# Weight decoding on Trainium2: the low bits and the sign share one word before the join

## The chip, the core and the metric

The kernel runs on one core of a Trainium2 chip. The metric is the device time of one execution in microseconds (us). The engines are TensorE (PE, with its weight loads PEld), VectorE (DVE), ScalarE (ACT), GpSimd (POOL) and SyncE (SP); transfers are issued from SP's and ACT's queues.

## The reference, cut to what matters

```python
out_up    = repeat(softmax(mean4(q) @ mean4(k).T * scale) @ mean4(v), 4)   # 4 x 8 heads, 576 tokens, 64 wide
out_local = softmax(where(abs(i - j) < 4, q @ k.T * scale, -1e9)) @ v
x = (out_up + out_local) as (2304 tokens, 512)
x = maximum(maximum(x @ w1, x @ w2), x @ w3) @ w_out      # 512 -> 768 -> 512
h = maximum(x @ w_in, 0); y = h * h @ w_out2              # 512 -> 2048 -> 512
```

q, k and v are 32-bit floats. All weights are 64-bit floats: a scale that is a 64-bit number multiplied them when they were drawn. The kernel receives them as 64-bit words.

## The kernel before, in words

**Decoding.** A weight block of 128x512 64-bit words (512 KB) is loaded into one of three buffers of the pool `stg` (tiles `raw_g` for w1 to w3, `raw_o` for the two output weights, `raw_f` for w_in; 18, 22 and 16 blocks, 56 in all). `raw_words` returns two views of it, the low and the high 32-bit words, each 128x512 at a step of 8 bytes. Then, by block:

- `rebias` (L108, DVE, one tensor operand and two constants) corrects the exponent in the high word;
- `low_bits` (L114, ACT) scales the low word so that its top three bits remain as a small integer;
- `join` issues two DVE instructions with two tensor operands each: L117 shifts the high word left by three, which drops its sign, and ors in the low bits; L120 takes the sign from the high word and ors it in. The low word now holds a 32-bit float.
- The float is split into a rounded part `hi` (ACT) and a remainder `lo` (DVE for w1 to w3, POOL for the others); each product on PE is three matmuls (`mm3`, L141 to L143: hi·hi, hi·lo, lo·hi).

**Stages.** Attention of batch 0 runs first, beside the decoding of w1 to w3; then, batch by batch, the gate units (`gate_unit`, PE into PSUM, DVE maximum `c` at L399), their output units, and the attention of the next batch. In the attention of batch b, `x32` (L352, DVE) takes the attention output of a pair of heads out of PSUM; `x3210F` is the one of batch 1, pair 0, front part. The last feed-forward block is cut into 24 units that the code calls quads: 3 token groups by 8 weight quads. In a quad PE computes seven products `P` (L141 to L143), from which DVE forms the sums `u` and `c` (L729, L737, L740, L744, L748), squares them (L714, L733) and subtracts (`gl`, L671); PE then multiplies these into `po`. `decode_quad` decodes four blocks (two `raw_f`, two `raw_o`) for one weight quad, forms four sums of them (L532 to L535) and stores the results for the later token groups; this is spread over the last batch and over the first token group, so that the quads from 465 to 568 us run beside it, and the later ones not.

**Order.** On PE the order is written by hand. On the other engines a scheduler orders the instructions at build time by a simulated timeline; at run time each engine takes its queue strictly in order, so an instruction that waits holds all behind it.

Of the kernel before, what the change touches and what calls it, by code (L numbers as in the profile page):

```python
# [7 lines left out]

F32 = mybir.dt.float32
F32R = mybir.dt.float32r  # L10
U32 = mybir.dt.uint32
U64 = mybir.dt.uint64
AF = mybir.ActivationFunctionType
ALU = mybir.AluOpType
# [7 lines left out]
LOW_BITS = 0.9375 * 2.0**-29  # L22
# [36 lines left out]
def local_global_attention__then__moe_kernel(  # L59
    ctx: ExitStack, tc: tile.TileContext, qT, kT, vP, cst, wg, wo1, wi2, wo2, out  # L60
):
    nc = tc.nc
# [38 lines left out]
    def raw_words(src, name):  # L101
        raw = stg.tile([P, 512], U64, tag="raw", name=f"raw_{name}")
        nc.sync.dma_start(out=raw, in_=src)
        words = raw.bitcast(U32).rearrange("p (n two) -> p n two", two=2)
        return words[:, :, 0], words[:, :, 1]

    def rebias(high):
        nc.vector.tensor_scalar(  # L108
            out=high.bitcast(F32), in0=high.bitcast(F32), scalar1=REBIAS, scalar2=F32_TOP,
            op0=ALU.mult, op1=ALU.min,  # L110
        )

    def low_bits(out, low):
        nc.scalar.activation(out=out, in_=low, func=AF.Copy, scale=LOW_BITS)  # L114

    def join(out, high, bits):
        nc.vector.scalar_tensor_tensor(  # L117
            out=out, in0=high, scalar=3, in1=bits, op0=ALU.logical_shift_left, op1=ALU.bitwise_or
        )
        nc.vector.scalar_tensor_tensor(  # L120
            out=out, in0=high, scalar=0x80000000, in1=out, op0=ALU.bitwise_and, op1=ALU.bitwise_or
        )

    def split_mid(items):
        parts = []
        work = [raw_words(src, name) for src, name, *_ in items]
        for (src, name, pool, tag, bufs), (low, high) in zip(items, work):
            rebias(high)
            low_bits(low, low)
            join(low, high, low)  # L130
            hi = pool.tile([P, 512], F32R, tag=tag, name=f"hi_{name}", bufs=bufs)
            lo = pool.tile([P, 512], F32R, tag=tag, name=f"lo_{name}", bufs=bufs)
            w = low.bitcast(F32)
            nc.scalar.activation(out=hi, in_=w, func=AF.Copy)
            eng = nc.gpsimd if wo_pool else nc.vector
            eng.tensor_tensor(out=lo, in0=w, in1=hi.bitcast(F32), op=ALU.subtract)
            parts.append((hi, lo))
        return parts
# [171 lines left out]
    def att_pv(b, p, part):  # L310
# [32 lines left out]
        if (b, h) not in x_t:  # L343
            assert not h or not b or all((b - 1, 1, f) in h_t for f in range(NF1))
            x_t[b, h] = (
                xp.tile([P, NP, N], F32R, tag=f"xhi{h}", name=f"xhi{b}{h}", bufs=2 - h),
                xp.tile([P, NP, N], F32R, tag=f"xlo{h}", name=f"xlo{b}{h}", bufs=2 - h),
            )
# [19 lines left out]
    def load_w1(n=2):  # L368
        keys = w1_todo[:n]
        del w1_todo[:n]  # L370
        items = [
            (wg[f, g], f"g{f}{g}", wpool, "w", 36) if kind == "g" else (wo1[f], f"o1{f}", wo_pool[0], "wo", 12)
            for kind, f, g in keys
        ]
        if items:
            w1_t.update(zip(keys, split_mid(items)))
# [16 lines left out]
    def gate_max(b, h, f, g, ps, c):  # L393
# [6 lines left out]
        if g == NG - 1:  # L400
            hhi = hp.tile([P, N], F32R, tag=f"hh{h}{f}", name=f"hh{b}{h}{f}")
            hlo = hp.tile([P, N], F32R, tag=f"hl{h}{f}", name=f"hl{b}{h}{f}")
            nc.scalar.activation(out=hhi, in_=c, func=AF.Copy)  # L403
# [76 lines left out]
    def quad_tiles(q):  # L480
        n = loads[0]
        loads[0] += 1
        t = w2_t[q] = {}
        for c in CUT:
            for e in "hl":
                if n % 4 == 3:
                    t[c + e] = gp.tile([P, 512], F32R, tag="w", name=f"w{n}{c}{e}", bufs=12)
                else:
                    t[c + e] = wpool.tile([P, 512], F32R, tag="w", name=f"w{n}{c}{e}", bufs=36)
        return t  # L490

    def split_cut(q, c, w, c0=0):
        n = w.shape[-1]
        hi, lo = w2_t[q][c + "h"][:, c0 : c0 + n], w2_t[q][c + "l"][:, c0 : c0 + n]
        nc.scalar.activation(out=hi, in_=w, func=AF.Copy)
        nc.gpsimd.tensor_tensor(out=lo, in0=w, in1=hi.bitcast(F32), op=ALU.subtract)

    def store_cut(q, c):
        n = 256 if c == "i3" else 512
        for e in "hl":  # L500
            nc.sync.dma_start(out=wscr[q][c + e], in_=w2_t[q][c + e][:, 0:n].bitcast(F32))

    def decode_quad(q):

        raw, tb = {}, {}

        def begin(key, src):
            low, high = raw[key] = raw_words(src, f"{key}_{q}")
            rebias(high)
            low_bits(low, low)  # L510

        def end(key):
            low, high = raw[key]
            join(low, high, low)
            raw[key], tb[key] = low.bitcast(F32), high.bitcast(F32)

        def both():
            quad_tiles(q)
            end("f0")
            split_cut(q, "i0", raw["f0"])  # L520

        def other():
            end("f1")
            split_cut(q, "i3", raw["f1"][:, 256:512])

        def sums():

            t1, t2 = tb["f0"][:, 0:256], tb["f0"][:, 256:512]
            t3, t4 = tb["f1"][:, 0:256], tb["f1"][:, 256:512]
            b11, b21 = raw["f0"][:, 0:256], raw["f0"][:, 256:512]  # L530
            b12, b22 = raw["f1"][:, 0:256], raw["f1"][:, 256:512]
            nc.vector.tensor_tensor(out=t1, in0=b12, in1=b11, op=ALU.subtract)  # L532
            nc.vector.tensor_tensor(out=t3, in0=b22, in1=b12, op=ALU.subtract)
            nc.vector.tensor_tensor(out=t2, in0=b22, in1=t1, op=ALU.subtract)
            nc.vector.tensor_tensor(out=t4, in0=t2, in1=b21, op=ALU.subtract)  # L535

        def last(c, key):
            end(key)
            split_cut(q, c, raw[key])

        def stores(*cuts):
            for c in cuts:
                store_cut(q, c)

        f = 2 * q
        return [
            lambda: begin("f0", wi2[f]),
            lambda: begin("f1", wi2[f + 1]),
            both,
            other,  # L550
            sums,
            lambda: (split_cut(q, "i1", tb["f0"]), begin("o0", wo2[f]), stores("i0", "i3")),
            lambda: (split_cut(q, "i2", tb["f1"]), begin("o1", wo2[f + 1]), stores("i1", "i2")),
            lambda: last("o0", "o0"),
            lambda: (last("o1", "o1"), stores("o0", "o1")),
        ]
# [275 lines left out]
```

## Time and profile before

| | |
|---|---|
| Median of 3 runs | 865.99 us (865.09 to 867.10) |
| The profiled execution | 864.85 us |
| Its span, first to last instruction | 863.1 us |
| PE busy | 809.9 us (94%) |
| DVE busy | 561.0 us (65%) |
| ACT, POOL busy | 298.5 us, 220.7 us |
| Mean granted TensorE clock | 0.972 |

The profile is read by stretches: the shares of the whole span average over a start in which PE has gaps, a long middle in which it has none, and the quads. A busy time is that of the instruction on its engine, with what it waits for a memory port included. Idle time is put down to the instruction that ended it. The granted clock is a share of full speed, where 1.0 is 2.4 GHz and 0.5 is 1.2 GHz.

### The profile page before, as it was taken

What the parts mean: (1) busy time and instruction counts of PE and PEld (TensorE: products, weight loads), DVE (VectorE), ACT (ScalarE), POOL (GpSimd) and SP (SyncE); (2) the same over time, 40 slices, a digit from 0 to 9 for tenths busy, and PEclk for the clock granted to TensorE, in tenths of its full rate; (3) what the DMA queues carried; (4) which work ended last, traced back from release to release, by engine and by line L of the source; (5) the groups of instructions that cost most, each with busy time, mean ns of one, the idle gap of its engine ahead of it and who ended that gap; (6) DMA issues with size and microseconds to landing.
All of it is one profiled execution on the core that took longest, in us unless ns stands there. A gap on an engine that the chain in (4) does not pass through costs nothing. (4 is left out here: it accounts for less than half of the span.)

```text
span 863.1 us, 15554 instructions
## 1 busy us (share of the span) xinstructions
PE 809.9 (94%) x6016; PEld 741.7 (86%) x6016; DVE 561.0 (65%) x1072; ACT 298.5 (35%) x679; POOL 220.7 (26%) x258
## 2 busy tenths in 40 slices
PE   5578997999999999999998988899999999999998
PEld 4367996999999999999998877788888898888886
DVE  7998998623764256638776998975654546544533
ACT  3455543422343123334445434424221123211211
POOL 4735383510433104103333344412000002000000
PEclk9578999999999999999999999999999999999999
DMA  8635542320223102135765766722564100654101
GB/s 246 209 105 171 162 144 73 120 66 2 73 84 94 35 27 82 32 106 195 232 231 167 281 219 244 249 92 77 194 209 155 50 1 24 207 196 134 49 1 73
DMA packets 66232, 110.30 MB, mean 128 GB/s; under 512 B 6800, under 2 KB 29680, under 8 KB 66160
## 3 DMA queue, kind: packets, MB, share of 16 engines
q1 hardware_dynamic: 61552, 104.60, 37.1%
q10 hardware_dynamic: 4608, 4.72, 1.6%
q8 instruction: 47, 0.77, 0.4%
q14 instruction: 25, 0.20, 0.1%
HBM read 76.79 MB, written 32.51 MB: 127 GB/s over the span
## 5 line engine op out<-in xcount | busy, mean ns | idle before, releaser
L141 PE MATMUL g<-xhi,hi_g 128*128 128x256 f32 (+1 forms) x576 | 175.6, 305 | 3.3 <-DVE c L399 3.2
L142 PE MATMUL g<-xlo,hi_g 128*128 128x256 f32 (+1 forms) x576 | 172.6, 300 | 1.5 <-DVE xlo L360 1.5
L143 PE MATMUL g<-xhi,lo_g 128*128 128x256 f32 (+1 forms) x576 | 172.5, 300 | 0.0
L141 PEld LDWEIGHTS g<-xhi,hi_g 128*128 128x128 f32 x576 | 111.1, 193 | 6.3 <-DVE c L399 4.9
L142 PEld LDWEIGHTS g<-xlo,hi_g 128*128 128x128 f32 x576 | 111.7, 194 | 1.7 <-DVE xlo L360 1.7
L143 PEld LDWEIGHTS g<-xhi,lo_g 128*128 128x128 f32 x576 | 110.9, 192 | 0.0
L670 ACT ACTIVATE gh<-c 128x384 fp32r<-128x384 f32 x96 | 50.3, 524 | 149.6 <-DVE c L714 133.0
L671 DVE TENSOR_TENSOR gl<-c,gh 128x384 fp32r<-128x384 f32 x96 | 62.2, 649 | 39.7 <-ACT gh L670 39.4
L399 DVE TENSOR_TENSOR c<-g,c 128x256 f32<-128x256 f32 (+1 forms) x96 | 43.5, 453 | 65.0 <-PE g L143 64.6
L141 PE MATMUL yp<-hh,hi_o 128*128 128x256 f32 (+1 forms) x192 | 58.8, 306 | 0.0
L143 PE MATMUL yp<-hh,lo_o 128*128 128x256 f32 (+1 forms) x192 | 57.5, 299 | 0.0
L142 PE MATMUL yp<-hl,hi_o 128*128 128x256 f32 (+1 forms) x192 | 57.5, 299 | 0.0
L403 ACT ACTIVATE hh<-c 128x256 fp32r<-128x256 f32 (+1 forms) x48 | 21.2, 442 | 95.0 <-DVE c L399 95.0
L714 DVE SCALAR_TENSOR_TENSOR c<-c 128x384 f32<-128x384 f32 x72 | 43.4, 604 | 1.9
L733 DVE TENSOR_TENSOR c<-c 128x384 f32<-128x384 f32 x24 | 15.7, 654 | 39.4 <-ACT c L732 39.4
L141 PEld LDWEIGHTS yp<-hh,hi_o 128*128 128x128 f32 x192 | 37.0, 193 | 0.8 <-issue 0.6
L610 POOL TENSOR_TENSOR lS<-s,hS 128x768 fp32r<-128x768 f32 x2 | 3.7, 1840 | 131.2 <-DVE u L729 115.8
L143 PEld LDWEIGHTS yp<-hh,lo_o 128*128 128x128 f32 x192 | 37.1, 193 | 0.0
L142 PEld LDWEIGHTS yp<-hl,hi_o 128*128 128x128 f32 x192 | 37.1, 193 | 0.0
L217 POOL TENSOR_TENSOR v<-v 72x256 f32<-72x256 f32 x32 | 26.0, 829 | 38.8 <-DMA v<-in_vP 38.8
L732 ACT ACTIVATE c<-P 128x384 f32<-128x384 f32 x24 | 11.8, 490 | 59.4 <-PE P L143 58.1
L405 DVE TENSOR_TENSOR hl<-c,hh 128x320 fp32r<-128x320 f32 (+1 forms) x36 | 19.9, 554 | 12.6 <-ACT hh L403 12.6
(1829 smaller groups left out, 2121.3 us busy)
## 6 DMA issues: line engine op xcount, KB each, us to landing
raw_o<-in_wo SPq DMA_DIRECT2D x22, 512.0 KB
raw_g<-in_wg SPq DMA_DIRECT2D x18, 512.0 KB
raw_f<-in_wi SPq DMA_DIRECT2D x16, 512.0 KB
k<-in_kT SPq DMA_DIRECT2D x16, 291.0 KB
q<-in_qT SPq DMA_DIRECT2D x16, 288.0 KB
v<-in_vP SPq DMA_DIRECT2D x32, 144.0 KB
out_y<-ob SPq DMA_DIRECT2D x18, 256.0 KB
vw<-in_vP SPq DMA_DIRECT2D x16, 175.0 KB
```

What stands on the lines that cost most here:

```text
L141: nc.tensor.matmul(ps, whi, xhi, start=first, stop=False, skip_group_check=more)
L142: nc.tensor.matmul(ps, whi, xlo, start=False, stop=False, skip_group_check=more)
L143: nc.tensor.matmul(ps, wlo, xhi, start=False, stop=last, skip_group_check=more)
L217: nc.gpsimd.tensor_tensor(out=v4[:, 0:2], in0=v4[:, 0:2], in1=v4[:, 2:4], op=ALU.add)
L399: nc.vector.tensor_tensor(out=c, in0=ps[:, 0:N], in1=c, op=ALU.max)
L403: nc.scalar.activation(out=hhi, in_=c, func=AF.Copy)
L405: eng.tensor_tensor(out=hlo, in0=c, in1=hhi.bitcast(F32), op=ALU.subtract)
L670: nc.scalar.activation(out=ghi, in_=c, func=AF.Copy)
L671: nc.vector.tensor_tensor(out=glo, in0=c, in1=ghi.bitcast(F32), op=ALU.subtract)
L714: V.scalar_tensor_tensor(out=c, in0=c, scalar=0.0, in1=c, op0=ALU.max, op1=ALU.mult)
L732: A.activation(out=e, in_=d, func=AF.Relu)
L733: V.tensor_tensor(out=e, in0=e, in1=e, op=ALU.mult)
```

## The change

`low_bits` now writes its three bits as a 16-bit number into the lower halfword of the low word, and a new DVE instruction with one tensor operand takes the sign bit from the upper halfword of the high word and writes it into the upper halfword of the low word. `join` is then one instruction: shift the high word left by three and or in the low word, which holds sign and low bits. The number of DVE instructions is the same: by block, one with two tensor operands (L120) is replaced with one with one tensor operand.

```diff
-    def low_bits(out, low):
-        nc.scalar.activation(out=out, in_=low, func=AF.Copy, scale=LOW_BITS)
-
-    def join(out, high, bits):
+    def low_bits(low, high):
+
+        half = lambda words, i: words.bitcast(U16)[:, :, i]
+        nc.scalar.activation(out=half(low, 0), in_=low, func=AF.Copy, scale=LOW_BITS)
+        nc.vector.tensor_scalar(
+            out=half(low, 1), in0=half(high, 1), scalar1=0x8000, scalar2=None, op0=ALU.bitwise_and
+        )
+
+    def join(low, high):
         nc.vector.scalar_tensor_tensor(
-            out=out, in0=high, scalar=3, in1=bits, op0=ALU.logical_shift_left, op1=ALU.bitwise_or
-        )
-        nc.vector.scalar_tensor_tensor(
-            out=out, in0=high, scalar=0x80000000, in1=out, op0=ALU.bitwise_and, op1=ALU.bitwise_or
+            out=low, in0=high, scalar=3, in1=low, op0=ALU.logical_shift_left, op1=ALU.bitwise_or
         )
...
-            low_bits(low, low)
-            join(low, high, low)
+            low_bits(low, high)
+            join(low, high)
...
-            low_bits(low, low)
+            low_bits(low, high)
...
-            join(low, high, low)
+            join(low, high)
```

Since the scheduler reckons with other durations, it also puts DVE's, ACT's, POOL's and SP's instructions into another order; PE's order is the same. In the changed file the lines behind the new code have numbers that are higher by three: L109 is `rebias`, L118 the new sign step, L123 the join, L355 `x32`, L402 the maximum.

DVE's queue just ahead of `x3210F`, before. `c013` and `c014` are maxima of gate units, `raw_f0_0`, `raw_f1_0` and `raw_o0_0` are blocks of weight quad 0:

```order
L534 TENSOR_TENSOR raw_f0_0_5421<-raw_f1_0_5425,raw_f0_0_5421 128x256
L108 TENSOR_SCALAR raw_o0_0_5549<-raw_o0_0_5549 128x512
L399 TENSOR_TENSOR c014_1706<-g0141_1708,c014_1706 128x320
L535 TENSOR_TENSOR raw_f1_0_5425<-raw_f0_0_5421 128x256
L117 SCALAR_TENSOR_TENSOR raw_o0_0_5549<-raw_o0_0_5549 128x512
L399 TENSOR_TENSOR c014_1706<-g0142_1722,c014_1706 128x320
L120 SCALAR_TENSOR_TENSOR raw_o0_0_5549<-raw_o0_0_5549 128x512
L352 TENSOR_TENSOR x3210F_1767<-o10F_1750,up10_1763 128x256
```

The same place now:

```order
L538 TENSOR_TENSOR raw_f1_0_5426<-raw_f0_0_5421 128x256
L277 TENSOR_TENSOR sm11B_1511<-sm11B_1511,sms11B_1528 128x350
L402 TENSOR_TENSOR c013_1649<-g0131_1651,c013_1649 128x320
L402 TENSOR_TENSOR c013_1649<-g0132_1665,c013_1649 128x320
L402 TENSOR_TENSOR c014_1706<-g0141_1708,c014_1706 128x320
L402 TENSOR_TENSOR c014_1706<-g0142_1722,c014_1706 128x320
L355 TENSOR_TENSOR x3210F_1767<-o10F_1750,up10_1763 128x256
```

The blocks of weight quad 0 have moved ahead, so that only maxima stand just before `x3210F`; in both orders 27 blocks are decoded ahead of it.

DVE's queue around the sum `u302` of the third quad (products of PE wait for it), before; `raw_o0_4` and `raw_o1_4` are blocks of weight quad 4:

```order
L733 TENSOR_TENSOR c1102_6451<-c1102_6451 128x384
L108 TENSOR_SCALAR raw_o1_4_6437<-raw_o1_4_6437 128x512
L120 SCALAR_TENSOR_TENSOR raw_o0_4_6412<-raw_o0_4_6412 128x512
L737 TENSOR_TENSOR u302_6479<-P7_02_6472,u202_6427 128x384
L117 SCALAR_TENSOR_TENSOR raw_o1_4_6437<-raw_o1_4_6437 128x512
```

The same place now:

```order
L109 TENSOR_SCALAR raw_o1_4_6438<-raw_o1_4_6438 128x512
L123 SCALAR_TENSOR_TENSOR raw_o0_4_6412<-raw_o0_4_6412 128x512
L736 TENSOR_TENSOR c1102_6453<-c1102_6453 128x384
L118 TENSOR_SCALAR raw_o1_4_6438<-raw_o1_4_6438 128x512
L740 TENSOR_TENSOR u302_6481<-P7_02_6474,u202_6428 128x384
L123 SCALAR_TENSOR_TENSOR raw_o1_4_6438<-raw_o1_4_6438 128x512
```

The rebias of `raw_o1_4` has moved ahead of `c1102`, and its sign step stands ahead of `u302`.

## Rows read from the trace of the kernel before

**Rows 1.** The page: busy time, granted clock, and the chain that ended last.

```profile
PE 809.9 (94%) x6016; PEld 741.7 (86%) x6016; DVE 561.0 (65%) x1072; ACT 298.5 (35%) x679; POOL 220.7 (26%) x258
...
PEclk9578999999999999999999999999999999999999
...
PE 31%; DVE 7%; DMA 4%; issue 2%; POOL 1%; ACT 1%; SPq 0%; DVEq 0%; POOLq 0%; ACTq 0%
```

**Rows 2.** Busy time by stretch (start:end length, each engine, PEclk, DMA share, GB/s).

```profile
20.00:40.00 20.00, 13.43 (x138) 9.99 (x136) 20.00 (x36) 10.51 (x25) 15.30 (x20) 0.50 0.64 190
...
120.00:140.00 20.00, 13.81 (x122) 12.06 (x120) 19.72 (x36) 8.06 (x19) 13.13 (x13) 1.00 0.30 105
...
480.00:520.00 40.00, 36.43 (x176) 31.15 (x175) 38.23 (x62) 17.18 (x32) 18.76 (x11) 1.00 0.68 234
520.00:560.00 40.00, 35.50 (x170) 30.00 (x169) 35.89 (x58) 17.76 (x32) 16.29 (x13) 1.00 0.71 249
...
640.00:680.00 40.00, 40.00 (x200) 35.96 (x199) 19.03 (x35) 8.24 (x16) 0.00 (x0) 1.00 0.49 158
```

**Rows 3.** The same view, two short stretches behind those.

```profile
140.00:145.00 5.00, 4.99 (x45) 4.57 (x45) 3.42 (x10) 2.19 (x9) 0.84 (x1) 0.66 0.01 2
560.00:570.00 10.00, 7.78 (x37) 6.31 (x36) 8.61 (x14) 3.75 (x7) 3.14 (x3) 1.00 0.56 174
```

**Rows 4.** PE in order of time, waits alone: start, length, instruction, [idle before <-releaser].

```profile
79.16 1.21 PE L298 MATMUL t03B<-const,sm03B 128*70 128x128 f32 x5 [3.53 <-ACT pt02B L282]
...
123.53 0.41 PE L141 MATMUL g<-xhi,hi_g 128*128 128x320 f32 x1 [0.49 <-DVE c L399]
126.19 0.41 PE L141 MATMUL g<-xhi,hi_g 128*128 128x320 f32 x1 [0.64 <-DVE c L399]
131.18 0.41 PE L141 MATMUL g<-xhi,hi_g 128*128 128x320 f32 x1 [1.20 <-DVE c L399]
139.66 0.30 PE L298 MATMUL t10B<-const,sm10B 128*70 128x128 f32 x1 [3.81 <-DVE x3210F L352]
...
502.85 0.45 PE L141 MATMUL P<-hA,w2i2h 128*128 128x384 f32 x1 [1.34 <-DVE u L737]
```

**Rows 5.** Durations by line, ns: shortest/median/longest, first and last start.

```profile
L117 DVE SCALAR_TENSOR_TENSOR raw_o<-raw_o x22: 643/694/1807, 102.3 to 565.8; 128x512 uint32<-128x512 uint32 x22
L120 DVE SCALAR_TENSOR_TENSOR raw_o<-raw_o x22: 678/688/1840, 106.1 to 567.3; 128x512 uint32<-128x512 uint32 x22
L108 DVE TENSOR_SCALAR raw_o<-raw_o x22: 416/423/1373, 99.7 to 565.2; 128x512 f32<-128x512 f32 x22
```

**Rows 6.** Busy time of line L120 alone, by stretch.

```profile
0.00:140.00 140.00, 23.05 (x27) 0.84 0.53 166
480.00:600.00 120.00, 12.62 (x16) 1.00 0.53 182
sum 600.00, DVE 47.86; mean DVE 11.97
```

**Rows 7.** Busy time of line L108 alone, in the same stretches.

```profile
0.00:140.00 140.00, 15.03 (x27) 0.84 0.53 166
480.00:600.00 120.00, 7.52 (x16) 1.00 0.53 182
sum 600.00, DVE 28.73; mean DVE 7.18
```

**Rows 8.** DVE in order of time, at a few places.

```profile
138.42 0.68 DVE L120 SCALAR_TENSOR_TENSOR raw_o<-raw_o 128x512 uint32<-128x512 uint32 x1
139.18 0.42 DVE L352 TENSOR_TENSOR x3210F<-o10F,up 128x256 f32<-128x256 f32 x1
...
501.30 0.43 DVE L108 TENSOR_SCALAR raw_o<-raw_o 128x512 f32<-128x512 f32 x1 [1.26 <-DMA raw_o<-in_wo]
```

**Rows 9.** SP's issue of a block, and ACT's first step on it.

```profile
90.25 0.33 SPq L103 DMA_DIRECT2D raw_g<-in_wg  x1
...
94.82 0.70 ACT L114 ACTIVATE raw_g<-raw_g 128x512 uint32<-128x512 uint32 x1 [2.34 <-DMA raw_g<-in_wg]
```

More of the change, by code (lines that the diff above doesn't have):

```diff
@@ L10 @@
 F32R = mybir.dt.float32r
+U16 = mybir.dt.uint16
 U32 = mybir.dt.uint32
```

## The prediction

> **What bounds the kernel now.** I read the page first, then busy time by stretch, then PE's waits in order of time, and last the durations of the lines that the change touches. PE is busy for 94% of the span [rows 1], so a step that DVE saves is worth something only where PE waits for DVE. The table by stretch shows where that is. From 20 to 40 us DVE is busy for all 20.00 us while PE has gaps, at a clock of 0.50 [rows 2]; from 120 to 140 us DVE is busy for 19.72 of 20 us and PE for only 13.81; from 480 to 560 us DVE is busy for 38.23 and 35.89 of 40 us and PE loses 3.57 and 4.50 us. In the later quads, without decoding, PE has no gap at all (40.00 of 40) and DVE is half idle [rows 2]. So three places can give time back: the start, the end of the first decoding around 120 to 140 us, and the quads beside which weight quads are decoded. The chain that ended last names DVE for 7% and DMA for 4% of the span [rows 1], more than any engine but PE.
>
> PE's waits in the second place are four: 0.49, 0.64 and 1.20 us for a maximum `c` and 3.81 us for `x3210F` [rows 4], **6.14 us** in sum. In the third, from 480 to 570 us, PE's gaps are 3.57 + 4.50 + (10 - 7.78) = **10.3 us** [rows 2, 3].
>
> **The change part by part.** *The removed step.* L120 takes 47.86 us for 56 blocks, 0.855 us each [rows 6]; its median is 0.69 us where no one disturbs it [rows 5], the rest is time in which POOL's work holds it up. 27 blocks are decoded by 140 us (23.05 us) and 16 from 480 to 600 us (12.62 us) [rows 6].
>
> *The new step.* No row shows a DVE step on 16-bit halves, or a bitwise step with one tensor operand. The nearest row is L108: one tensor operand and constants, 128x512 elements at the same step of 8 bytes, median 0.42 us and 28.73 us in all, 0.513 each [rows 5, 7]. The farthest is L117, bitwise on the same words with two tensor operands, 0.69 us by median [rows 5], 0.855 if it is held up as L120 is. I take L108, since the number of tensor operands is what parts these two rows, and keep 0.42 to 0.855 for the range. The saving on DVE is then 23.05 - 15.03 = **8.0 us** by 140 us and 12.62 - 7.52 = **5.1 us** in the quads [rows 6, 7].
>
> The excess over the median is 0.17 us for L120 (0.855 - 0.69) and 0.09 us for L108 (0.513 - 0.42), and which of the two the new step has is open [rows 5 to 7]. The Trainium skill ("SBUF — State Buffer", SBUF: two separate sides) says that DVE and GpSimd share a port pair as an exclusive lock, held for a whole instruction, both by DVE steps with two SBUF operands and by one-operand steps in the fast mode; what a blocked step waits would then depend on POOL's instruction and not on its own length. By that rule the new step costs 0.42 + 0.17 = 0.59 us as an estimate, saves 0.265 us instead of 0.34, and the sum below falls from 8.8 to about 8.2 us.
>
> *Waits.* The new step overwrites half of the word that ACT's low_bits reads, so it waits for ACT, as L117 did before it; behind it in the queue stands what stood behind L117. In the order the rebias is followed directly by the next decoding step of its block 11 times before and 14 times now. Such a place can make DVE wait for the rest of ACT's step; three more of them, some 0.3 us each (ACT's step and the sign step start with the same landing), stay below 1 us and are in the bounds. ACT's step is the same but for 16-bit output; no row shows that, and ACT, at 35% [rows 1], has room: bounds 0 and a loss of some tenths per block that lies beside DVE's queue.
>
> *Order, start to 100 us.* The scheduler fills the time it saves with the next block: up to `x3203F` 9 sign steps and 10 rebiases stand ahead where 8 second joins and 9 rebiases did, and summing medians over the queue, `x3203F` and the last `xlo` of that part stand within 0.8 us of where they stood. What PE waits for there does not come sooner. I charge **0**, with +3.5 us if the wait of 3.53 us at 79 us [rows 4] goes, and -2.5 us if blocks land too late (below).
>
> *Order, 120 to 140 us.* In both orders 27 blocks stand ahead of `x3210F`, now with nothing but maxima just before it. DVE had no idle time there to speak of, so `x3210F` can come 8.0 us sooner, more than the 6.14 us that PE waits. Then PE's own work is next. I take **5.5 us** of the 6.14, as one maximum in the row will still be waited for. Bounds: 4, and 7.8 if the stretch behind it, at a clock of 0.66 for 5 us [rows 3], runs at full clock too (5 x 0.34 = 1.7 us).
>
> *160 to 460 us.* PE has no gaps to speak of; 13 blocks get cheaper beside it: 0.
>
> *The quads.* DVE saves 5.1 / 16 = 0.32 us per block [rows 6, 7]. But at four places DVE stands idle until a block lands, as at 501.30 us, 1.26 us, right ahead of the `u` for which PE then waits 1.34 us [rows 4, 8]; what is saved ahead of such a place goes into that wait. So 12 of 16 blocks: 3.8 us. At this very place the order is worse now: behind the landing stand a join's 0.69, a `c`'s 0.55 and the sign step's 0.42 ahead of `u302`, where the join alone stood; about 1 us, which I charge by half, since the load may be issued sooner: **3.3 us** of the 10.3. Bounds: 0 and 8.
>
> The sum is 0 + 5.5 + 3.3 = 8.8 us. Against the profiled execution (864.85 us, span 863.1) that is 856.05; the median of the runs is 1.14 us above that execution, so **857.2 us** for the median, 1.0% less.
>
> **The rivals.** *Only one term comes.* The start's gain can be lost to a late attention step, or the quads' to the loads. 865.99 - 5.5 = 860.5 or - 3.3 = 862.7; say 861.5.
>
> *Both stretches cease to wait.* If DVE falls behind PE's need in both, all of 6.14 + 1.7 and most of 10.3, and some of the start, come back: some 18 us, 848. For it: without decoding, quads show no gap. Against: DVE is busy for 74.1 of the 80 us from 480; 5.1 less is 69, against PE's 71.9 [rows 2, 6, 7], so the two stay neck and neck and waits remain.
>
> *The new step is no faster.* If a bitwise step on halves runs like L117, DVE saves nothing and only the order changes: 866, plus or minus 2. The Trainium skill ("Vector Engine (DVE) Microarchitecture Reference", 5.1) lists streams with steps above 2 as not measured, which is this step's case.
>
> *Slower: blocks land too late.* Three buffers; a block's load is issued when the remainder `lo` of the third block ahead is done, and lands some 4.6 us later: issued at 90.25, first used at 94.82 after a wait [rows 9]. By medians, DVE's work between that `lo` and the rebias was 5.0 us on average and is now 4.5, at the least 3.0. DVE then waits at the head of its queue, and softmax and `xlo` steps wait behind it while PE waits for them. It decides from 0.5 us per block on (18 blocks, 9 us, eat the sum); at 0.8 us it is a loss of 5 to 6 us: 871.
>
> **How the numbers follow.** Forecast 0.50 (853 to 860 by itself), one term only 0.16, both stretches 0.10, no faster step 0.13, slower 0.11. A measurement of this kernel tells about 0.2% (1.7 us) from no change: below 864.3 is faster, above 867.7 slower. Faster: 0.50 + 0.16 + 0.10 + 0.03 of the step that is no faster = 0.79; same 0.10, the rest of it; slower 0.11. The range from 849.5 to 866.0 leaves out the slower case and most of the greatest gain.
>
> **What would show it.** The new line at 0.42 to 0.6 us by its median (right), at 0.69 or more (wrong); DVE's busy time lower by about 19 us (47.86 - 28.73). PE's wait for `x3210F` gone, and the busy time of PE in the 20 us around it near 19. The gaps of PE in the decoding quads near 7 us instead of 10.3. DVE idle for `raw_g` before 100 us, which is none now, would show the slower case at work. The prediction falls if POOL's hold on DVE grows as DVE's steps crowd, or if PE's clock in the start is granted differently.

## The result and the profile after

The changed kernel is slower: 876.66 us median of 4 runs (876.18 to 878.89), where the kernel before took 866.22 us (865.09 to 867.10, 4 runs). The ratio is 1.0142, with an interval of 1.0126 to 1.0158; the quotient of the two medians is 1.0121, a little below it. The highest run of the kernel before is 9 us under the lowest of the changed one, so the loss is clear of the noise. The forecast was 857.2 us in a range of 849.5 to 866.0, so it had the sign wrong and missed by 19.5 us. The profiled execution took 876.61 us with a span of 874.8 us, 11.7 us more than before.

The page shows where the two new steps stand. First busy time, answering [rows 1]:

```profile
PE 813.7 (93%) x6016; PEld 743.1 (85%) x6016; DVE 559.2 (64%) x1072; ACT 330.4 (38%) x679; POOL 223.4 (26%) x258
```

DVE's busy time fell by 1.8 us where 19 were expected, and ACT's rose by 31.9 us where next to nothing was. The new lines by duration (ns: shortest/median/longest, first and last start), answering [rows 5]; L117 is now ACT's `low_bits` and L118 the sign step:

```profile
L117 ACT ACTIVATE raw_o<-raw_o x22: 1346/1382/1409, 94.1 to 572.6; 128x512 uint16<-128x512 uint32 x22
...
L118 DVE TENSOR_SCALAR raw_o<-raw_o x22: 732/752/1278, 96.5 to 574.0; 128x512 uint16<-128x512 uint16 x22
L118 DVE TENSOR_SCALAR raw_g<-raw_g x18: 723/822/1682, 17.0 to 91.6; 128x512 uint16<-128x512 uint16 x18
L118 DVE TENSOR_SCALAR raw_f<-raw_f x16: 719/750/772, 124.1 to 560.4; 128x512 uint16<-128x512 uint16 x16
```

The sign step, at 0.75 us, is no cheaper than the step it replaces (0.69) [rows 5], and ACT's step has doubled, from 0.70 us [rows 9] to 1.38.

Busy time in the stretches of [rows 2, 3] (start:end length, each engine, PEclk, DMA share, GB/s):

```profile
20.00:40.00 20.00, 13.41 (x140) 10.20 (x142) 19.71 (x38) 13.20 (x27) 15.01 (x18) 0.50 0.62 184
120.00:140.00 20.00, 16.56 (x110) 15.90 (x110) 15.33 (x33) 7.98 (x14) 13.08 (x12) 0.91 0.25 89
480.00:520.00 40.00, 35.94 (x175) 30.96 (x174) 39.27 (x61) 21.47 (x30) 13.81 (x11) 1.00 0.76 265
520.00:560.00 40.00, 35.05 (x160) 27.61 (x158) 33.25 (x57) 20.90 (x32) 13.79 (x11) 1.00 0.68 236
...
560.00:570.00 10.00, 9.27 (x45) 7.84 (x45) 9.66 (x16) 5.39 (x10) 5.93 (x4) 1.00 0.44 140
```

From 120 to 140 us PE has fewer gaps than before (16.56 us busy for 13.81), but its work there comes some 2 us later (`x3210F` starts at 141.2 us, where it started at 139.18 [rows 8]). From 480 to 570 us PE's gaps are 4.06 + 4.95 + 0.73 = 9.7 us, where 10.3 stood and near 7 was forecast, but the quads start later too. A stretch of fixed times therefore says little across kernels, and three marks in PE's own work say more: the last output of attention (`o33B`), the first matmul of the quads (`P<-hA,w0i0h`) and the first that reads weight quad 4 (`P<-hA,w4i0h`). PE in order of time, start and length, at these marks, before and then after:

```profile
381.14 0.39 PE L334 MATMUL o33B<-ptd33B,vd 72*64 72x48 f32 x8
462.52 0.34 PE L141 MATMUL P<-hA,w0i0h 128*128 128x384 f32 x1
597.37 0.33 PE L141 MATMUL P<-hA,w4i0h 128*128 128x384 f32 x1
```

```profile
381.57 0.39 PE L337 MATMUL o33B<-ptd33B,vd 72*64 72x48 f32 x8
468.88 0.34 PE L144 MATMUL P<-hA,w0i0h 128*128 128x384 f32 x1
608.31 0.33 PE L144 MATMUL P<-hA,w4i0h 128*128 128x384 f32 x1
```

So of the 11.7 us, 0.4 were lost by the first mark, 87.31 - 81.38 = 5.9 between the first and the second, 139.43 - 134.85 = 4.6 between the second and the third, and 0.8 behind it. Half of the loss lies where the forecast charged 0 ("160 to 460 us ... 0"): PE had gaps of 0.4 us in the 60 us from 400 before, and has 6.1 us of them now. Busy time in that stretch, before and then after:

```profile
400.00:460.00 60.00, 59.62 (x442) 58.95 (x441) 44.47 (x77) 26.12 (x52) 19.36 (x15) 1.00 0.69 228
```

```profile
400.00:460.00 60.00, 53.91 (x396) 52.41 (x396) 39.26 (x66) 29.40 (x46) 19.83 (x15) 1.00 0.62 213
```

What happens there is seen on DVE in order of time (start, length, instruction, [idle before <-releaser]); `c` (L402) is the maximum of the gate units, for which PE waits five times in these 60 us, 5.9 us in sum:

```profile
410.11 0.43 DVE L109 TENSOR_SCALAR raw_f<-raw_f 128x512 f32<-128x512 f32 x1 [1.93 <-DMA raw_f<-in_wi]
411.52 0.76 DVE L118 TENSOR_SCALAR raw_f<-raw_f 128x512 uint16<-128x512 uint16 x1 [0.98 <-ACT raw_f L117]
412.07 0.45 DVE L402 TENSOR_TENSOR c<-g,c 128x256 f32<-128x256 f32 x1
...
418.26 1.28 DVE L118 TENSOR_SCALAR raw_o<-raw_o 128x512 uint16<-128x512 uint16 x1
419.34 0.51 DVE L402 TENSOR_TENSOR c<-g,c 128x320 f32<-128x320 f32 x1
```

The first three rows are one block: it lands, its rebias takes 0.43 us, ACT's step takes 1.39 us from the same landing, and DVE stands idle for 0.98 us at the sign step, with the maximum behind it. PE did not yet wait for this maximum; it waited 0.81 us for the next one, at 416.22 us. The other two rows show a later maximum behind a sign step of 1.28 us, and PE's wait for it is 1.41 us:

```profile
419.90 0.42 PE L144 MATMUL g<-xhi,hi_g 128*128 128x320 f32 x1 [1.41 <-DVE c L402]
```

Over the whole run, DVE's idle time ahead of L118 (the last column; busy us and mean ns stand in front of it) is 7.0 + 4.6 + 0.6 = 12.2 us for ACT alone:

```profile
L118 DVE TENSOR_SCALAR raw_o<-raw_o 128x512 uint16<-128x512 uint16 x22 | 18.2, 828 | 4.8 <-ACT raw_o L117 4.6
L118 DVE TENSOR_SCALAR raw_g<-raw_g 128x512 uint16<-128x512 uint16 x18 | 16.7, 926 | 0.7 <-ACT raw_g L117 0.6
L118 DVE TENSOR_SCALAR raw_f<-raw_f 128x512 uint16<-128x512 uint16 x16 | 12.0, 749 | 7.7 <-ACT raw_f L117 7.0 <-DVE raw_f L109 0.5
```

Before, the step that waited for ACT was the first join (L117), and it stood idle for 1.5 + 0.2 us:

```profile
L117 DVE SCALAR_TENSOR_TENSOR raw_o<-raw_o 128x512 uint32<-128x512 uint32 x22 | 20.2, 919 | 0.4 <-ACT raw_o L114 0.2
L117 DVE SCALAR_TENSOR_TENSOR raw_f<-raw_f 128x512 uint32<-128x512 uint32 x16 | 12.9, 806 | 2.0 <-ACT raw_f L114 1.5
```

Among PE's longest waits by 140 us, answering [rows 4], these are new:

```profile
28.04 1.04 PE L309 MATMUL td01F<-const,pd01F 128*72 128x128 f32 x4 [3.50 <-DVE x3200F L355]
...
46.26 0.58 PE L145 MATMUL g<-xlo,hi_g 128*128 128x256 f32 x1 [2.81 <-DVE xlo L363]
55.27 0.58 PE L145 MATMUL g<-xlo,hi_g 128*128 128x256 f32 x1 [2.29 <-DVE xlo L363]
...
129.26 0.52 PE L144 MATMUL g<-xhi,hi_g 128*128 128x320 f32 x1 [3.34 <-ACT c L400]
```

The wait for `x3210F` (3.81 us) is gone, as forecast. In its place stand waits for `x3200F` and the remainders `xlo` in the start, and one of 3.34 us for a `c` that ACT writes. They are not what the dearer steps cost. The kernel with both steps on whole words (below), which has the same order of instructions, has them too (us in total, times, longest):

```profile
PE g L145 <- DVE xlo L363: 8.3, 3, 3.2
PE td01F L309 <- DVE x3200F L355: 4.0, 1, 4.0
PE g L144 <- ACT c L400: 2.8, 1, 2.8
```

So up to 140 us the new order mostly trades one set of waits for another, whatever the steps cost.

### The profile page after: what moved, and what is told of

Its sections match the earlier page's. It is cut to its first block, busy times and chain, and to the rows that moved or that the text cites. A ratio compares the mean times of both kernels' runs of the same rounds, so it can differ in the third digit from the quotient of the medians.

```text
span 874.8 us, 15590 instructions
## 1 busy us (share of the span) xinstructions
PE 813.7 (93%) x6016; PEld 743.1 (85%) x6016; DVE 559.2 (64%) x1072; ACT 330.4 (38%) x679; POOL 223.4 (26%) x258
## 5 line engine op out<-in xcount | busy, mean ns | idle before, releaser
L402 DVE TENSOR_TENSOR c<-g,c 128x256 f32<-128x256 f32 (+1 forms) x96 | 43.6, 454 | 65.6 <-PE g L146 65.2
L674 DVE TENSOR_TENSOR gl<-c,gh 128x384 fp32r<-128x384 f32 x96 | 59.4, 619 | 39.8 <-ACT gh L673 39.7
L717 DVE SCALAR_TENSOR_TENSOR c<-c 128x384 f32<-128x384 f32 x72 | 46.2, 642 | 2.0
L117 ACT ACTIVATE raw_o<-raw_o 128x512 uint16<-128x512 uint32 x22 | 30.4, 1381 | 25.2 <-DMA raw_o<-in_wo 23.3
```

Source lines behind the costliest of these rows:

```text
L117: nc.scalar.activation(out=half(low, 0), in_=low, func=AF.Copy, scale=LOW_BITS)
L402: nc.vector.tensor_tensor(out=c, in0=ps[:, 0:N], in1=c, op=ALU.max)
L674: nc.vector.tensor_tensor(out=glo, in0=c, in1=ghi.bitcast(F32), op=ALU.subtract)
L717: V.scalar_tensor_tensor(out=c, in0=c, scalar=0.0, in1=c, op0=ALU.max, op1=ALU.mult)
```

## The experiments

Theory 1 says that the prices of the two steps are the cause: ACT's half words hold up the head of DVE's queue, and the sign step is as dear as what it replaced. Theory 2 says that the scheduler's new order is the cause, whatever the steps cost. Theory 3 blames the sign step on halves alone.

**A table of single steps.** Six of each, 128x512 elements:

> A table of single steps, six of each, without any of the layer's computation (it leaves all of it out; its time says nothing). In the changed kernel the sign step takes 0.72 to 0.75 us where 0.42 was charged, and ACT's low bits 1.35 us where 0.69 stood before. If writing half a word beside its other half is what costs, then the same step with a contiguous output of half words is near 0.42 (VectorE) and near 0.69 (ACT), and with a contiguous input but the halves as output stays at 0.72 and 1.35. If reading half words costs on VectorE, it is the other way round: contiguous output 0.72, contiguous input 0.42. If only the spacing of 8 bytes counts, the halves at a spacing of 4 bytes are near 0.42 and 0.69. The whole-word form of the sign step (the words at a spacing of 8 bytes on both sides) gives 0.42 if halves are dearer than words, and 0.7 if they are not.

Groups by line (busy us, mean ns, idle before). In the first fence, the first four are ACT's halves or bytes, by the spacing of the output: 8 bytes (L61, and L65 for single bytes), 4 bytes (L72), contiguous (L75); then ACT's whole words at 8 bytes (L59) and contiguous (L70).

```profile
L65 ACT ACTIVATE vb<-vb 128x512 uint8<-128x512 uint32 x6 | 8.0, 1333 | 0.2
...
L61 ACT ACTIVATE vb<-vb 128x512 uint16<-128x512 uint32 x6 | 7.9, 1320 | 0.0
L72 ACT ACTIVATE g<-vb 128x512 uint16<-128x512 uint32 x6 | 5.0, 828 | 0.0
...
L75 ACT ACTIVATE g<-vb 128x512 uint16<-128x512 uint32 x6 | 4.2, 692 | 0.0
L59 ACT ACTIVATE vb<-vb 128x512 uint32<-128x512 uint32 x6 | 4.1, 679 | 16.4 <-DMA vb<-in_w 16.4
...
L70 ACT ACTIVATE g<-vb 128x512 uint32<-128x512 uint32 x6 | 4.0, 660 | 0.0
```

For DVE: halves at 8 bytes on both sides (L43), contiguous input to halves at 8 bytes (L49), halves at 8 bytes to a contiguous output (L47), halves at 4 bytes on both sides (L55), contiguous words (L53), words at 8 bytes (L45), contiguous halves (L51).

```profile
L43 DVE TENSOR_SCALAR va<-va 128x512 uint16<-128x512 uint16 x6 | 4.4, 728 | 1.5 <-DMA va<-in_w 1.5
L49 DVE TENSOR_SCALAR va<-d 128x512 uint16<-128x512 uint16 x6 | 4.3, 711 | 0.0
...
L47 DVE TENSOR_SCALAR d<-va 128x512 uint16<-128x512 uint16 x6 | 2.7, 458 | 0.0
L55 DVE TENSOR_SCALAR d<-e 128x512 uint16<-128x512 uint16 x6 | 2.7, 448 | 0.0
L53 DVE TENSOR_SCALAR e<-d 128x512 uint32<-128x512 uint32 x6 | 2.6, 433 | 0.0
L45 DVE TENSOR_SCALAR va<-va 128x512 uint32<-128x512 uint32 x6 | 2.5, 412 | 0.0
L51 DVE TENSOR_SCALAR e<-d 128x512 uint16<-128x512 uint16 x6 | 1.7, 278 | 0.0
```

It is the writing of halves at a spacing of 8 bytes that costs, on both engines: on DVE 0.71 us even from a contiguous input, and 0.46 when only the input is spaced; on ACT 1.32 for 0.69. Whole words at the same spacing cost nothing extra (0.41 and 0.68), and at 4 bytes most of the price is gone (0.45 and 0.83, for 0.28 and 0.69 contiguous).

**Two by two: halves or words on each engine.** All three kernels keep the changed kernel's order of instructions. The first one undoes ACT's part:

```diff
-        nc.scalar.activation(out=half(low, 0), in_=low, func=AF.Copy, scale=LOW_BITS)
+        nc.scalar.activation(out=low, in_=low, func=AF.Copy, scale=LOW_BITS)
```

> The changed kernel with one thing undone: ACT writes the three low bits as a whole word, as in the kernel before; the sign step then overwrites the upper half. Same order of instructions on every engine as the changed kernel. Theory 1 (ACT's output of halves, 0.69 us longer a block, holds up the head of VectorE's queue): ACT's busy time falls by 32 us, and the time to 864 to 868, within 0.3% of the kernel before, as the sign step of 0.75 us is as dear as the step that the change took out. Theory 2 (the new order of instructions loses the time, whatever the steps cost): about 875, no change. Theory 3 (VectorE's sign step on halves loses it): 873 or more, as that step is left as it is.

The second one puts the sign step on whole words as well, and the third only that:

```diff
         nc.vector.tensor_scalar(
-            out=half(low, 1), in0=half(high, 1), scalar1=0x8000, scalar2=None, op0=ALU.bitwise_and
+            out=low, in0=high, scalar1=0x80000000, scalar2=None, op0=ALU.bitwise_and
         )
```

> The changed kernel with both new steps on whole words: ACT writes the three low bits as a whole word, and VectorE then writes the sign over the whole word instead of its upper half. This leaves the three low bits out of every weight. Same order of instructions as the changed kernel. It gives the price at which the prediction's sum was made, if a whole-word step costs 0.42 us: theory 1 expects the sum to hold then, 857 us (853 to 860); theory 2 (the new order) expects 872 or more; if the whole-word step also takes 0.7 us or more, theory 1 expects the time of the kernel before, 864 to 868.

> The changed kernel with VectorE's sign step on the whole word, and ACT's output of half words as changed. This leaves the three low bits out of every weight. Same order of instructions as the changed kernel. Theory 1 (ACT's 1.38 us holds up the head of VectorE's queue; the sign step's price is some 8 us of the sum): 870 (867 to 873), still slower than the kernel before. Theory 3 (the sign step on halves is what loses the time): 859 or less. Theory 2 (the order): 875. With the first two kernels it makes a table of two by two: if the parts add, the time here is that of the changed kernel plus that of whole words on both, less that of ACT on whole words alone.

The last two of these leave the three low bits out of every weight. The first row of the table was measured beside runs of the kernel before with a median of 866.22 us, the other three beside runs with 865.26 us:

| ACT writes | sign step on | us | against before, with interval |
|---|---|---|---|
| halves | halves (the change) | 876.66 | 1.0142 (1.0126 to 1.0158) |
| words | halves | 869.62 | 1.0045 (1.0029 to 1.0060) |
| halves | words | 868.97 | 1.0035 (1.0015 to 1.0054) |
| words | words | 859.60 | 0.9936 (0.9918 to 0.9954) |

Theory 1 holds in its parts. By the medians ACT's halves cost 7.0 us with the sign step on halves and 9.4 us with it on words; the sign step's halves cost 7.7 and 10.0 us. By the ratios it is 0.97% and 0.99%, and 1.07% and 1.09%, some 8 to 9 us each, with intervals of some 0.2% on each ratio: as far as these runs tell, the two parts add. Both together make 17.1 us of the 19.5 by which the forecast was off. By the traces ACT's part goes through the head of DVE's queue, as theory 1 has it: with ACT on words and all else as changed, DVE's idle time for ACT ahead of the sign step falls from 12.2 to 2.1 us, while its other waits for ACT sum to 139.4 us with halves and 141.2 with words, and PE's own waits for ACT to 11.7 and 10.7. Theory 2 as the main cause falls, since the same order gives a gain of 0.64% at the price that the sum was made with. Theory 3 falls as well: with the sign step on words and ACT on halves the kernel is still slower than before. The first kernel was expected within 0.3% of before and came out at 0.45%; some 4 us were not in theory 1. The second (expected at 853 to 860 us) and the third (867 to 873) came out within what theory 1 said.

**The same edits in the order of before.** If the sign step is written with two inputs, the scheduler keeps the order of before:

```diff
-        nc.vector.tensor_scalar(
-            out=half(low, 1), in0=half(high, 1), scalar1=0x8000, scalar2=None, op0=ALU.bitwise_and
+        nc.vector.scalar_tensor_tensor(
+            out=half(low, 1), in0=half(high, 1), scalar=0x8000, in1=half(high, 1), op0=ALU.bitwise_and, op1=ALU.bitwise_and
         )
```

> The arithmetic of the changed kernel with ACT writing whole words, and the sign step written as an instruction with two inputs (the upper half of the high word and itself): the scheduler then puts every instruction where it stands in the kernel before. So it is the kernel with ACT on whole words and the sign step on halves, in the order of before. That kernel in the changed order took 1.0045 of before. If the new order is what cost those 0.45%, this one is at 1.000 (0.998 to 1.002), provided that the step takes about the 0.7 us of the step that it replaces; if the order costs nothing and the halves do, it is at 1.004 to 1.006.

> As the run with ACT on whole words in the order of before, with ACT's output in half words as in the changed kernel, still in the order of before. In the changed order ACT's halves cost 7.0 us (876.66 against 869.62) with the sign step on halves and 9.4 us (868.97 against 859.60) with it on whole words. If that is a matter of ACT's price alone, it is 7 to 10 us here too, 1.008 to 1.012 of before. If the new order is what exposes ACT's step (the sign step right behind the rebias at the head of VectorE's queue, waiting for ACT), it is 0 to 4 us here, 1.000 to 1.005.

Measured: 887.00 us with ACT on words, 1.0227 (1.0200 to 1.0254), and 892.89 us with ACT on halves, 1.0309 (1.0285 to 1.0334). The proviso of the first expectation did not hold: with two inputs the step on halves takes about twice the 0.7 us (1.32 to 1.33 us by its medians, more on average, as the groups of the run with ACT on words show), so neither of its branches was tested.

```profile
L118 DVE SCALAR_TENSOR_TENSOR raw_o<-raw_o 128x512 uint16<-128x512 uint16 x22 | 34.3, 1558 | 0.5 <-ACT raw_o L117 0.3
L118 DVE SCALAR_TENSOR_TENSOR raw_g<-raw_g 128x512 uint16<-128x512 uint16 x18 | 27.5, 1529 | 0.0
```

The pair still says what ACT's halves cost in the order of before: 5.9 us by the medians, which lies between the two branches of the second expectation (0 to 4 and 7 to 10 us), and 0.82%, some 7 us, by the ratios. The next run asks the same with the steps of before. Besides ACT's output it edits the shift, which is the first of the two join instructions and not the second:

```diff
-        nc.scalar.activation(out=out, in_=low, func=AF.Copy, scale=LOW_BITS)
+        nc.scalar.activation(out=out.bitcast(U16)[:, :, 0], in_=low, func=AF.Copy, scale=LOW_BITS)
...
-            out=out, in0=high, scalar=3, in1=bits, op0=ALU.logical_shift_left, op1=ALU.bitwise_or
+            out=out, in0=high, scalar=3, in1=bits, op0=ALU.logical_shift_left, op1=ALU.bitwise_and
```

> The kernel before with one thing changed: ACT writes the three low bits as a half word (into the lower half of the low word). Its second join masks with the low word where it was joined with it, to keep the values finite: the weights it decodes are wrong, the steps and their order are those of before. It gives ACT's price alone. 1.008 to 1.012 of before if 0.69 us more for a block on ACT hold up what waits for ACT wherever it stands; 1.000 to 1.005 if the new order is needed to expose it. ACT's busy time should rise by 56 x 0.65 to 0.69 = 36 to 39 us, or 32 as in the changed kernel.

Measured: 871.63 us, 1.0048 (1.0026 to 1.0071), so ACT's halves alone cost 0.48%, some 4.2 us, in the order of before, and ACT's busy time rose from 298.5 to 331.7 us. That lies at the edge of the lower branch. DVE's idle time for ACT ahead of the first join grew from 1.7 to 5.9 + 2.7 + 0.7 = 9.3 us. ACT's price is thus paid in either order, 4 to 7 us in the old and 7 to 9 us in the new one. The new order is not needed for it; whether it adds to it is not shown, since the steps differ too and the intervals nearly meet.

**Where the parts fall.** The three marks of PE's work in the profiled executions (start of `o33B`, then the time to the first matmul of the quads, to the first on weight quad 4, and to the end of the span), as differences from before in us:

| kernel | to `o33B` | to the quads | to weight quad 4 | to the end | span |
|---|---|---|---|---|---|
| halves, halves (the change) | +0.4 | +5.9 | +4.6 | +0.8 | +11.7 |
| words, halves | -2.6 | +2.4 | +1.4 | +1.4 | +2.5 |
| halves, words | -1.9 | +5.6 | -0.4 | +1.2 | +4.4 |
| words, words | -3.6 | +1.6 | -2.9 | +0.8 | -4.1 |
| before, ACT on halves | +1.8 | +1.8 | +2.4 | +1.0 | +7.0 |

Each row is one execution, and the executions of one kernel spread by up to 7 us (865.29 to 872.27 for words and halves, of which the profiled one took 867.44), so a difference of 1 to 2 us in one row is not shown by it alone. ACT's halves cost 2 to 4 us in each of the first three parts, in the new order (first row less the second, third less the fourth) most of all ahead of the quads (3.5 and 4.0). The sign step's halves cost 4.3 us in the third part on their own. And every kernel in the new order is at least 1.6 us later between `o33B` and the quads, with cheap steps too; PE's waits in that part sum to 0.9 us before and to 2.7 in the kernel with words on both. DVE's rows, before and then in that kernel, show the likely place: before, the maximum stood ahead of the join of `raw_o`, and now the sign step stands ahead of the maximum:

```profile
415.18 0.48 DVE L399 TENSOR_TENSOR c<-g,c 128x320 f32<-128x320 f32 x1
415.58 0.88 DVE L117 SCALAR_TENSOR_TENSOR raw_o<-raw_o 128x512 uint32<-128x512 uint32 x1
```

```profile
413.29 0.97 DVE L118 TENSOR_SCALAR raw_o<-raw_o 128x512 uint32<-128x512 uint32 x1
414.17 0.48 DVE L402 TENSOR_TENSOR c<-g,c 128x320 f32<-128x320 f32 x1
```

PE waited 1.19 us for the second of these maxima, and not for the first. That the order costs these 1.6 to 2.4 us is argued from such rows; no run here changes the order alone, and it stays open.

**A version that keeps every bit and pays neither price.** From the table of steps: ACT writes whole words into a tile of their own, contiguous, the sign goes into the upper halves of that tile (a spacing of 4 bytes), and the join reads them from there.

```diff
+        bits = stg.tile([P, 512], U32, tag="bits", name=f"bits_{name}", bufs=2)
+        upper = bits.bitcast(U16).rearrange("p (n two) -> p n two", two=2)[:, :, 1]
-        nc.scalar.activation(out=half(low, 0), in_=low, func=AF.Copy, scale=LOW_BITS)
+        nc.scalar.activation(out=bits, in_=low, func=AF.Copy, scale=LOW_BITS)
         nc.vector.tensor_scalar(
-            out=half(low, 1), in0=half(high, 1), scalar1=0x8000, scalar2=None, op0=ALU.bitwise_and
+            out=upper, in0=high.bitcast(U16)[:, :, 1], scalar1=0x8000, scalar2=None, op0=ALU.bitwise_and
         )
```

> A version that could beat both. In the table of single steps a half word written at a spacing of 4 bytes took 0.45 us on VectorE against 0.73 at 8 bytes, and ACT's whole words took 0.66 us into a contiguous tile. Here ACT writes its low bits as whole words into a tile of their own, the sign goes into the upper half of that tile's words, and the join reads them there; nothing is left out. There is room for two such tiles only if the raw weights have two buffers where they had three. If the price of the steps is what counts, as in the kernel with both steps on whole words (0.9936 of before), 0.993 to 0.997. If the third raw buffer is needed to load ahead (VectorE's first step already waits some 16 us for raw weights in the kernel before), slower than before: 1.005 to 1.02, with a wait of the first step for its DMA that has grown by 10 us or more.

Measured: 874.21 us, 1.0094 (1.0062 to 1.0126). That is the slower of the two outcomes that were expected, and for the reason given there: the third raw buffer is needed. The rebias now waits 22.6 + 5.5 + 19.1 = 47 us for blocks to land, where it waited 8.5 + 4.7 = 13 us before.

```profile
L109 DVE TENSOR_SCALAR raw_o<-raw_o 128x512 f32<-128x512 f32 x22 | 10.9, 497 | 22.8 <-DMA raw_o<-in_wo 22.6
L109 DVE TENSOR_SCALAR raw_g<-raw_g 128x512 f32<-128x512 f32 x18 | 9.3, 515 | 5.8 <-DMA raw_g<-in_wg 5.5
L109 DVE TENSOR_SCALAR raw_f<-raw_f 128x512 f32<-128x512 f32 x16 | 8.8, 552 | 21.1 <-DMA raw_f<-in_wi 19.1 <-POOL w1i0l L500 1.8
```

So the tiles were made only for the 32 blocks of the quads, where there is room once the attention's pool is closed, and the other 24 blocks keep the in-place form with ACT on whole words. Three of the 32 had their sign step by 130 us in the changed kernel; now the first sign step into such a tile comes at 379.8 us, so the start is lighter by the decoding of three blocks. Two tiles fit if the accumulators `c` have one buffer fewer:

```diff
-    tmp = p1.enter_context(tc.tile_pool(name="tmp", bufs=4, side="right"))
+    tmp = p1.enter_context(tc.tile_pool(name="tmp", bufs=3, side="right"))
...
+        bits_pool.append(ctx.enter_context(tc.tile_pool(name="qb", bufs=1, reuse_waits="tile")))
...
-            low_bits(low, high)
+            raw[key] = low, high, low_bits_apart(low, high, f"{key}_{q}")
```

> Nothing left out. Up to the quads as the kernel with ACT on whole words and the sign step on halves in place; in the quads (32 of the 56 blocks) ACT writes its low bits as whole words into a tile of their own, and the sign goes into the upper half of its words, at a spacing of 4 bytes, so 0.46 us a block for 0.75 to 0.8. Two such tiles fit once the attention is over, if the accumulators c have three buffers where they had four; the raw weights keep their three. If the sign step's price in the quads is what cost time: DVE's busy time 32 x 0.3 = some 10 us less than with halves in place (556), and the time below the 1.0045 of before that this one gave, at 0.994 to 1.000. If the price counts in the start alone (where the granted clock came back sooner in the kernels with the cheap step), 1.002 to 1.006. If the fourth accumulator is needed, PE waits for c longer between 140 and 460 us, and it is 1.005 or more.

> As the version with two tiles for the low bits in the quads, with one tile for them and the four accumulators of the kernel before. ACT's low bits of the next block then wait for the join of the last one. If that wait lies beside other work, the same as the version with two tiles or a little better, 0.993 to 1.000 of before; if it holds up the head of VectorE's queue, the sign step's idle time before it grows from 3 us to 10 us or more and the time is 1.002 to 1.010 of before.

> As the version with two tiles in the quads, but with the two joins of the kernel before (whole words, two inputs) up to the quads, so the start is that of before apart from the order that the scheduler makes of it. Nothing left out. If the halves in place cost time in the start (0.8 us against 0.7 to 0.85 of the removed step), it is 1 to 3 us faster than the version with halves there; if the start is as fast with either, they agree within 1 us.

| tiles in the quads | blocks ahead of the quads | us | against before (864.95 us), with interval |
|---|---|---|---|
| two | sign on halves in place | 860.95 | 0.9950 (0.9931 to 0.9968) |
| one | sign on halves in place | 865.92 | 1.0007 (0.9988 to 1.0027) |
| two | the two joins of before | 861.83 | 0.9961 (0.9941 to 0.9981) |

With two tiles the kernel is faster than both the kernel before and the changed one, with nothing left out. The sign step there takes 0.50 us with what disturbs it, for 0.75 to 0.83 in the changed kernel:

```profile
L128 DVE TENSOR_SCALAR bits_f<-raw_f 128x512 uint16<-128x512 uint16 x16 | 8.0, 502 | 1.6 <-ACT bits_f L127 1.3
L128 DVE TENSOR_SCALAR bits_o<-raw_o 128x512 uint16<-128x512 uint16 x16 | 7.9, 496 | 1.6 <-ACT bits_o L127 1.3
```

Against the kernel with words and halves in place (1.0045) the tiles are worth some 0.9%, with the lighter start, one accumulator fewer and some moves in the order in it; of the 7.9 us between the two profiled spans, 4.9 lie between the second and the third mark. One tile is too few: the kernel gives back the gain and lies just above the faster of its two expected ranges. The likely cause is that ACT's next block waits for the join of the last one; that wait fell on ACT, ahead of its own step (7.5 us), and not ahead of the sign step as expected (2.4 us there). It is not shown to be the cause, since the order and the number of accumulators differ as well. The last row keeps the joins and, up to the quads, nearly the order of before, and agrees with the first within 0.9 us: in this lighter start, the new order and the halves in place together cost nothing that these runs can tell.

## Why the prediction was wrong, point by point

- **What bounds the kernel** was right: a cheaper step in DVE's queue does give time back. At the price of the sum DVE's busy time is 540.9 us, 20.1 less (19 was forecast), and the kernel takes 859.60 us (0.9936 of before), where the forecast was 857.2 (0.990 of before). That this is so near is in part luck, as the terms below did not all come as they were charged.
- **The new step** was mis-sized, and this is one half of the miss. The number of tensor operands was taken to be what sets the price, and so the row of L108 (0.42 us). The whole-word form of the step does take 0.41 us, but the halves take 0.73 undisturbed, so DVE's busy time fell by 1.8 us instead of 19. The rival "the new step is no faster" had this half, at 0.13, and was chosen against for want of a row on halves. Its own time, 866 plus or minus 2, was missed by some 10 us for the second half; with ACT on words it is 869.62, nearly that.
- **The excess over the median**: 46.9 us for 56 blocks is 0.84 us each, 0.11 over the undisturbed 0.73, between the 0.09 and the 0.17 that were weighed. In the kernel with words on both the sign step took 10.8 + 9.5 + 8.1 = 28.4 us, 0.51 each, which is 0.09 over its median, as in the row of L108. Either value was small beside the 0.3 us of price. The Trainium skill ("SBUF — State Buffer", SBUF: two separate sides) describes a port pair that DVE and GpSimd share as an exclusive lock; the 0.59 us that the prediction worked out with it, as an estimate, was too much for the step that it was made for (0.51).
- **ACT's step** was the other half. "bounds 0 and a loss of some tenths per block that lies beside DVE's queue" failed twice: the loss was 0.69 us a block, and it did not lie beside DVE's queue. The prediction had itself written that the sign step waits for ACT and what stands behind it, and costed that wait at less than 1 us with ACT's old 0.69 us. With 1.38 us it is 12.2 us of idle time at the head of DVE's queue, and 7 to 9 us of the total. A low share of busy time (35%) says that an engine has room; it does not say that nobody waits for the end of its step.
- **The start to 100 us, charged at 0**: the wait of 3.53 us at 79 us did shrink to 0.45, but new ones for `x3200F` (3.50 us) and `xlo` (2.81 and 2.29 us) came in its place.
- **120 to 140 us**: the reordering did take away the wait for `x3210F`, but not for the reason given: it is gone with no cheaper step at all, and a wait for ACT's `c` of 2.6 to 3.5 us stands nearby in all four kernels of the table of two by two. The kernel with words and halves reaches `o33B` 2.6 us sooner than before in its profiled execution, and with cheap words 3.6 us sooner, where the term was 5.5.
- **The quads**: 3.3 was forecast for the price of 0.42, and the kernel at that price gained 2.9 between the second and third mark (one execution). This term was about right in size and fell with the price: in the changed kernel it is a loss of 4.6.
- **160 to 460 us, charged at 0**, was wrong with cheap steps as well (+1.6 us), and +5.9 in the changed kernel. PE without gaps was read as cover, but DVE's maxima come just in time there, and a sign step or a wait ahead of them can open a gap.
- **The slower rival** (blocks land too late) ended on the right side by the wrong mechanism: DVE's idle time for `raw_g` is 0.5 us in the changed kernel. That two buffers are too few was seen when one of the three was taken away.
- **The granted clock in the start** was named as a risk. In the stretch from 20 to 40 us it was 1.00 in the kernel with words on both and 0.50 in the one with two tiles, and both reached `o33B` at 377.5 us; but the second has the lighter start, so that pair does not settle it. The runs of the kernel before tell more: beside the experiments it ran 52 times, with a mean granted clock either up to 0.974 or from 0.985 on, and the first group took 0.7 to 1.0 us longer on average in each of the three sets. The changed kernel ran at 0.970 to 0.980. By that the clock explains about 1 us, as an estimate, and not the 10 that were lost.

## What to carry to other kernels

A change of element size is a change of price, even where the number of elements, the operation and the spacing stay as they are: a step that no row shows should be costed with all that it changes (operands, element size, spacing of the output), and the range should reach to the dearest of them on each engine that the edit touches. A step on an idle engine is on the path as soon as another engine's queue waits for its end; ask how long that wait is if the step doubles. And a stretch in which PE has no gaps is cover only for work that does not stand ahead of what PE takes next.

## What the runs showed of the hardware

Writing 16-bit elements at a spacing of 8 bytes took 1.32 us on ACT against 0.69 contiguous, and 0.71 to 0.73 us on DVE against 0.28; on ACT single bytes were the same (1.33). On DVE with two inputs the halves took 1.31 to 1.33 us (medians by kind of block) for 0.67 to 0.69 on words. Reading halves at that spacing cost much less (0.46 us to a contiguous output). Whole words at a spacing of 8 bytes took 0.41 us on DVE, no more than contiguous ones (0.43). The Trainium skill ("Vector Engine (DVE) Microarchitecture Reference", 5.2 Measured stream behaviour on trn2) says that a stream runs at its full rate only in runs of two or more adjacent 4-byte words; for these one-input steps on words the table of single steps does not agree, and the measurement decides.
